# A new hand-written order of all operations, setup copies on either of two engines, and other operands for the fill matmuls

## The chip, the cores and the metric

The kernel runs on one core of a Trainium2 chip. The core has five engines that work through their own instruction streams and wait for one another by semaphores: TensorE (PE in the profile, its weight loads PEld), VectorE (DVE), ScalarE (ACT), GpSimd (POOL) and SyncE (SP), which here issues nearly all DMAs. The metric is the device time of one execution in microseconds (us); a median over runs is compared.

## The reference, cut to what matters

```python
def reference(A_u, A_*, B_*):
    x = A_u                                             # (1, 2048, 512), bf16
    h = x + S4(layernorm(x))                            # state-space convolution
    return h + mlp(layernorm(layernorm(h)))             # 512 -> 1376 -> 512

def S4(u, A, B, C, log_dt, Dskip):                      # A, B, C: complex (512, 128)
    dt = exp(log_dt)
    P = exp(dt * A[:, :, None] * arange(2048))          # arange is rounded to bf16
    K = einsum("dn,dnl,dn->dl", C, P, dt * B).real      # one kernel of 2048 taps per channel
    y = irfft(rfft(pad(u)) * rfft(pad(K)))[:2048]       # long convolution over time
    return y + u * Dskip

def mlp(y, w1, b1, w2, b2):
    return gelu(y @ w1 + b1) @ w2 + b2
```

So: 512 kernels of 2048 taps are generated from 128 complex modes each, 2048 rows are convolved with them, and an MLP of 2 x 2048 x 512 x 1376 multiply-adds follows.

## The kernel before, in words

**Setup (0 to about 45 us).** The six parameter arrays are loaded and transposed by TensorE. VectorE computes phases and logarithms of 512 channels x 128 modes in small operations; ScalarE takes exponentials of them (L724, `bexps`; L941 and L944, `aexps`, out of PSUM). GpSimd builds constants: the scaled identities `WA` (one 128x128 tensor_scalar each, 20 of them), index tables by iota and memset, and `W2`. SyncE copies the split phases into the stacked array `S2` (`restack`, 16 DMAs of 32 KB). VectorE also takes the layer norm statistics of the 16 row tiles (`BN_STATS`, L863). When ScalarE has done its last exponential it loads another function table (L501) and turns to sines.

**Kernel generation (about 45 to 97 us).** `chain` adds up phases in PSUM (L978), ScalarE takes sines of them (L980), and VectorE multiplies the exponentials by them (L999, L1000, and L985, L986 for the second half of the channels). GpSimd meanwhile masks the tables `W` (28 tensor_scalars of 128x4x32), `DD` (128x32) and others, all through the helper `PTS` (L558, recorded at L555). `kgen` (L1022, L1023) contracts over the modes for the first half of the channels; its result gets the skip weight added by VectorE (L1036), which reads `Dz`. `Dz` is loaded by four tiny DMAs on SyncE (`in_A_Dskip`, L1180). One more DMA on SyncE, of 768 KB (`ar<-ar 128x8x384`), copies padding from `EA2` to `IA2`; it may start when GpSimd has done its masks, since temporaries lie where it writes.

**Spectra (about 97 to 160 us).** `kspec` (L1087), `kgen4` (L1053, L1054), `xspec` (L885) and `fstage` (L904) are matmuls whose results ScalarE (L507) or VectorE (L509) copy out of PSUM. `kstage` sends a transposed copy through DRAM (`AK_d`). `inverse` multiplies the spectra on VectorE (L1127), transforms back on TensorE (L1137) and turns the result by a DMA transpose (L1143).

**Tail and MLP (about 160 us to the end).** `tail` (L1201, L1206) adds the residual, takes the second layer norm's statistics on VectorE (L1214, then a chain of 128x4 operations at L553 to L569), scales, and transposes (L1239); `mlp` does L1260 with a GELU on ScalarE (L1262), and L1282 with an addition on VectorE (L1284) and the output DMAs.

**What sets the order.** Every operation is recorded as an `Op` with its engines, a modelled cost and its operands. `Sched.run` walks through the list `ORDER`, a table of numbers that says in which order the 1045 operations are issued and, by a sign, on which of two engines one runs. Engines execute their own instructions in that order. `run` keeps modelled times, and where it models TensorE idle it inserts fill matmuls (`fill`, L1370 to L1372), which write a free PSUM slot. `LAG`, `OWN` and the costs at the `add` calls are the model's numbers. The key `hv` marks an operation that takes part in a mutual stop of GpSimd and VectorE. Before, a VectorE operation so marked is lengthened by a marked GpSimd operation; GpSimd is never lengthened.

Of the kernel before, what the change touches and what calls it, by code (L numbers as in the profile page):

```python
# [9 lines left out]
ACT = mybir.ActivationFunctionType  # L10
# [140 lines left out]
class VS(V):  # L151
# [12 lines left out]
LAG = {"PE": 0.12, "ACT": 0.20, "DVE": 0.14, "POOL": 0.15, "SP": 0.15}  # L164
OWN = {"PE": 0.0, "ACT": 0.17, "DVE": 0.11, "POOL": 0.1, "SP": 0.0}
ORDER = [
# [78 lines left out]
class Sched:  # L245
# [42 lines left out]
    def run(self, nslots):  # L288
        ops = self.ops
        left = {}  # L290
        for o in ops:
            for p in set(o.ps):
                left[p] = left.get(p, 0) + 1
        free = dict(FREE)
        clk, pf, lands = Clock(), 0.0, []
        slots = [0.0] * nslots
        taken = [None] * nslots
        dma_busy, bulk = 4.0, 4.0
        ipe, blk = 16, 0.0
        order, seen = [], set()  # L300
        assert sorted(i if i >= 0 else ~i for i in ORDER) == list(range(len(ops)))
# [77 lines left out]
def kernel(ctx, tc, A_u, A_A_re, A_A_im, A_B_re, A_B_im, A_C_re, A_C_im, A_log_dt, A_Dskip,  # L379
# [18 lines left out]
    pe = Pe()  # L398
# [1014 lines left out]
```

## Time and profile before

| | |
|---|---|
| median of 3 runs | 273.55 us (273.02 to 274.47) |
| the profiled execution's own time | 274.52 us |
| its span, first to last instruction | 272.7 us |
| PE busy | 234.8 us (86%), 3237 matmuls |
| DVE busy | 181.4 us (67%) |
| ACT busy | 176.8 us (65%) |
| POOL busy | 70.2 us (26%), all but one instruction in the first 86 us |
| chain that ended last | PE 57%, POOL 15%, DVE 12%, ACT 8%, DMA 4% |
| mean granted TensorE clock | 0.969 of full speed |

The chain that ended last is followed back from the last instruction, at each step to what released it. Shares of busy time are averages over stages with different limits; which engine a stage waits for is read stage by stage.

### The profile page before, as it was taken

Reading aid. Unit: us, or ns where it says so; the run is one execution under the profiler, and the core shown is the slowest. Engines: PE = TensorE matmul, PEld = TensorE weight load, DVE = VectorE, ACT = ScalarE, POOL = GpSimd, SP = SyncE. Lnnn points to the kernel's source line nnn. Section 1 sums busy time; section 2 is a strip of 40 time slices with the busy share of each in tenths; the row PEclk is TensorE's granted clock in tenths of the full one; section 3 lists DMA queues with packets and bytes.
Section 4 is the critical chain, followed back from the end, with each engine's and each line's share of the span. In section 5 each row is a group of like instructions: output and inputs, shape, how many; then the busy total and the mean of one; then the engine's idle time right before and its main releaser. Section 6 shows DMA issues by size and latency. Waiting matters only on the chain.

```text
span 272.7 us, 7643 instructions
## 1 busy us (share of the span) xinstructions
PE 234.8 (86%) x3237; PEld 134.3 (49%) x3237; DVE 181.4 (67%) x351; ACT 176.8 (65%) x214; POOL 70.2 (26%) x251
## 2 busy tenths in 40 slices
PE   6319948977885499999999988899999999999994
PEld 2206723444764358643447753655654444444452
DVE  3889996999992584278699883799538662412021
ACT  3899929999792587789899861885531561451810
POOL 8968613999996000000000000000000000000000
PEclk9999997999999599999999995999999999999999
DMA  5660010100002108696476999041254004106302
GB/s 158 158 129 11 17 48 5 3 4 2 5 2 69 54 0 266 186 306 184 144 242 183 173 155 215 2 81 25 55 102 83 19 9 80 38 0 136 78 5 72
DMA packets 40371, 23.88 MB, mean 88 GB/s; under 512 B 25649, under 2 KB 37778, under 8 KB 40338
## 3 DMA queue, kind: packets, MB, share of 16 engines
q1 hardware_dynamic: 39746, 22.95, 34.9%
q8 instruction: 25, 0.41, 0.6%
q10 hardware_dynamic: 592, 0.46, 0.6%
q14 instruction: 8, 0.07, 0.1%
HBM read 10.03 MB, written 6.29 MB: 60 GB/s over the span
## 4 chain that ended last, share of the span: by engine, by line
PE 57%; POOL 15%; DVE 12%; ACT 8%; DMA 4%; issue 2%; SPq 1%; ACTq 0%; DVEq 0%; POOLq 0%
PE ps L1260 14%; PE ps L1282 14%; POOL ar L555 13%; PE ps L1137 7%; PE ps L885 5%; PE ps L904 5%; ACT ar L507 4%; PE ps L1087 3%; DVE ar L863 3%; DVE ar L564 3%; DVE ar L569 2%; PE ps L1206 2%; DMA ar<-ar 2%; PE ps L1053 2%; DVE ar L555 2%
## 5 line engine op out<-in xcount | busy, mean ns | idle before, releaser
L507 ACT CAST ar<-ps 128x1024 bf16<-128x1024 f32 (+3 forms) x75 | 66.6, 961 | 18.9 <-DVE ar L1214 6.8
L1262 ACT ACTIVATE ar<-ps,ar 128x512 bf16<-128x512 f32 (+1 forms) x44 | 28.3, 684 | 42.3 <-PE ps L1260 41.1
L555 POOL TENSOR_SCALAR ar<-ar 128x128 bf16<-128x128 bf16 (+6 forms) x60 | 46.7, 799 | 0.4
L980 ACT ACTIVATE ar<-ps 128x1024 bf16<-128x1024 int16 x36 | 34.7, 1029 | 12.0 <-DVE ar L1000 7.2
L1260 PE MATMUL ps<-ar 128*128 128x512 bf16 (+1 forms) x176 | 40.1, 380 | 0.0
L1282 PE MATMUL ps<-ar 128*128 128x512 bf16 (+3 forms) x187 | 39.8, 367 | 0.0
L509 DVE CAST ar<-ps 128x1024 bf16<-128x1024 f32 (+3 forms) x25 | 28.7, 1162 | 15.0 <-PE ps L885 5.1
L978 PE MATMUL ps<-ar 128*32 128x256 f16 x560 | 23.2, 293 | 16.4 <-ACT ar L980 12.2
L1284 DVE TENSOR_TENSOR ar<-ps,ar 128x512 bf16<-128x512 f32 (+1 forms) x17 | 11.1, 658 | 37.1 <-PE ps L1282 19.7
L1127 DVE TENSOR_TENSOR ar<-ar 128x1024 bf16<-128x1024 bf16 x48 | 30.6, 686 | 6.3 <-PE ps L1137 6.2
L1282 PEld LDWEIGHTS <-ar 128*128 128x128 bf16 (+1 forms) x187 | 18.0, 97 | 20.3 <-issue 1.0
L978 PEld LDWEIGHTS <-ar 128*32 128x32 f16 x560 | 15.0, 101 | 25.1 <-issue 19.6
L1260 PEld LDWEIGHTS <-ar 128*128 128x128 bf16 (+1 forms) x176 | 17.3, 100 | 20.3 <-issue 0.6
L1137 PE MATMUL ps<-ar 64*128 64x128 bf16 x768 | 25.4, 223 | 1.3 <-ACT ar L507 1.1
L1137 PEld LDWEIGHTS <-ar 64*128 64x128 bf16 x768 | 22.9, 98 | 6.7 <-issue 4.0
L904 PE MATMUL ps<-ar 128*64 128x512 bf16 (+1 forms) x160 | 17.8, 342 | 0.9 <-ACT ar L507 0.8
L576 ACT ACTIVATE ar<-ar 128x512 f32<-128x512 f32 (+8 forms) x18 | 11.9, 687 | 8.6 <-DVE ar L569 5.4
L724 ACT ACTIVATE ar<-ar 128x1024 bf16<-128x1024 f32 x16 | 15.8, 1044 | 1.0 <-DVE ar L553 1.0
L885 PE MATMUL ps<-ar 128*32 128x512 bf16 x256 | 16.0, 381 | 0.0
L933 PE MATMUL ps<-ar 128*128 128x512 f16 x24 | 8.0, 460 | 8.4 <-DVE ar L553 7.4
L999 DVE TENSOR_TENSOR ar<-ar 128x1024 bf16<-128x1024 bf16 x21 | 15.0, 737 | 0.2
L569 DVE SCALAR_TENSOR_TENSOR ar<-ar 128x4 f32<-128x4 f32 (+5 forms) x44 | 12.6, 288 | 3.7 <-ACT ar L576 2.9
(100 smaller groups left out, 320.6 us busy)
## 6 DMA issues: line engine op xcount, KB each, us to landing
ar<-AK_d SPq DMA_DIRECT2D x8, 512.0 KB, 6.5
ar<-in_A_u_dram SPq DMA_DIRECT2D x4, 512.0 KB, 7.7
AK_d<-ar SPq DMA_DIRECT2D x2, 1024.0 KB, 5.5
AK_d<-ar SPq DMA_DIRECT2D x4, 512.0 KB, 3.7
out_dram<-ar SPq DMA_DIRECT2D x30, 64.0 KB, 2.1
ar<-in_B_w_dram SPq DMA_DIRECT2D x4, 344.0 KB, 5.3
ar<-in_B_w_dram SPq DMA_DIRECT2D x2, 640.0 KB, 4.9
ar<-ar SPq DMA_DIRECT2D x1, 768.0 KB
```

Source lines behind the costliest of these rows:

```text
L507: act.copy(out_fn(), in_fn())
L509: dve.tensor_copy(out_fn(), in_fn())
L555: en.tensor_scalar(a, b, f(s1), f(s2), op0, op1)
L885: pe.matmul(pst(p)[32 * cg:32 * cg + 32, 512 * z:512 * z + 512], lhsT=BD.ap()[:, 32 * f + 2 - 2 * jl:32 * f + 34 - 2 * jl], rhs=un[2 * (2 ...
L904: pe.matmul(pst(p)[64 * h:64 * h + 64, w * (k + r):w * (k + r) + w], lhsT=T.ap()[:, f, r, :], rhs=v[f:f + 1].ap()[:, 0, :], start=True, st ...
L978: pe.matmul(pst(p)[32 * g:32 * g + 32, 256 * j:256 * j + 256], lhsT=W2[DELTAS.index(d)].ap(), rhs=S2[g].ap()[:, ch0:ch0 + 256], start=Fals ...
L980: add("ACT", c_act(1024), lambda e, p=p, sc=sc, cs=cs: act.activation(swo(sc[cs]) if hf and kind == "B" else sc[cs].ap().rearrange("p a b ...
L1127: dve.tensor_tensor(o, a, b_[:, :, ::-1, :] if sw else b_, ALU.mult)
L1137: pe.matmul(pst(p)[:, 512 * h + 128 * k:512 * h + 128 * k + 128], lhsT=q.ap()[rows, 2 * k + r, :], rhs=TP[w].ap()[rows, f0 // 2 + k, :], s ...
L1260: pe.matmul(pst(p)[:fs, 512 * z:512 * z + 512], lhsT=w1s[dc].ap()[:, fc * P:fc * P + fs], rhs=ybuf.ap().rearrange("p (t c) k -> p c t k", ...
L1262: add("ACT", c_act(512, 1), lambda e, p=p, z=z, fc=fc, fs=fs: act.activation(hT.ap()[:fs, fc, :], pst(p)[:fs, 512 * z:512 * z + 512], ACT. ...
L1282: pe.matmul(pst(p)[:, 512 * z + c0:512 * z + c1], lhsT=hT.ap()[:fs, fc, 128 * t:128 * t + 128], rhs=w2s[fc].ap()[:fs, c0:c1], start=(fc == ...
```

## The change

- `ORDER` is replaced as a whole. Many setup operations that stood on GpSimd alone may now stand on VectorE, and the new table puts 17 of them there: 11 of the 20 scaled identities `WA`, one index table of 128x512, four of the 28 masks `W`, and one 128x512 subtraction (`HLg[1]`). Two copies out of PSUM of `kgen` and one of 128x512 in the setup go from VectorE to ScalarE.
- The model in `run` changes: a marked GpSimd operation now also waits for a VectorE operation under way, and pushes VectorE's next; PE's lag is 0.19 for 0.12, a DMA transpose costs 2.5 for 2.2. This acts on the instructions only through where fills are inserted: 42 instead of 30.
- Fills multiply `identb` by the raw input rows `hs[15]` throughout, as soon as both are there; before, they multiplied `I16` by a constant, and later `identb` by `TP[0]`.

```diff
-LAG = {"PE": 0.12, "ACT": 0.20, "DVE": 0.14, "POOL": 0.15, "SP": 0.15}
+LAG = {"PE": 0.19, "ACT": 0.20, "DVE": 0.14, "POOL": 0.15, "SP": 0.15}
 ORDER = [
-    15, 0, 146, 1, 11, 12, 2, 16, 28, 4, 60, 183, 155, 3, 17, 61, 18, 83, 19, 82, 63, 62, 65, 98, 64, 147, 84, 76, 5, 72, 20, 99, 8, 85, 42, 39, 104,
...
+    15, 12, 0, 1, 6, 2, 11, 60, 145, 3, 61, 183, 63, 62, 16, 65, -57, 113, 5, -44, 83, -38, 13, 185, 84, 4, 114, -48, 85, 49, 115, -52, 116, -51, 64,
...
-            if e == "DVE" and o.hv and pf > s:
-                end += min(2.6, pf - s)
+            if e == "DVE" and o.hv:
+                end += min(2.6, max(0.0, pf - s))
+                hold = hold[-15:] + [(s, end)]
             if e == "POOL" and o.hv:
-                pf = end
-            if e == "PE" and s > FILL0 and s - free[e] > 0.6 and fs:
-                t, z = max(fs[0][0], free[e], FILL0), fs[0][1]
+                for a, b in hold:
+                    if a <= s < b:
+                        s, end = b, b + c
+                late = [a for a, _ in hold if s < a < end]
+                free["DVE"] += min(2.6, end - late[0]) if late else 0.0
+                o.start, pf = s, end
+            if e == "PE" and self.src <= seen and s - free[e] > 0.6 and fs:
+                t, z = max([fs[0][0], free[e], FILL0] + [ops[d].end + 0.2 for d in self.src]), fs[0][1]
...
-                    dma_busy = max(share(end, 2.2, bulk), dma_busy)
+                    dma_busy = max(share(end, 2.5, bulk), dma_busy)
...
-        add(eng, c_dve(n, mode, psum) if eng == "DVE" else 0.25 + n / 1540.0, fn, r=r, w=[o], pr=pr, hv=1)
+        c = c_dve(n, mode, psum) + (0.08 if isinstance(s1, V) else 0.02)
+        add("DVE" if eng == "DVE" else ("POOL", "DVE"), c if eng == "DVE" else (0.25 + n / 1540.0, c), fn, r=r, w=[o], pr=pr, hv=int(not psum))
...
-    def fill(z, t):
-        w, x = (I16.ap(), cst.ap()) if t < 60 else (identb.ap(), TP[0][0:4].ap().rearrange("p a b -> p (a b)"))
-        pe.matmul(slots[z][:, 0:512], lhsT=w, rhs=x, start=True, stop=True)
+    def fill(z):
+        pe.matmul(slots[z][:, 0:512], lhsT=identb.ap(), rhs=hs[15].ap(), start=True, stop=True)
```

Lines of the changed file are 6 to 8 higher than those of before (L519 becomes L525, L1180 becomes L1188, L1127 becomes L1135).

**SyncE's queue from the restacks to the first copy to DRAM.** `ar<-ar 32x512` is a restack, `in_A_Dskip` a quarter of `Dz`, `in_B_b` the bias, `ar<-ar 128x8x384` the padding, `AK_d` the spectrum. Before:

```order
L519 DMA ar<-ar 32x512 x15
L1180 DMA ar<-in_A_Dskip_dram 1x4x32
L1180 DMA ar<-in_B_b_dram 128x10x1
L1180 DMA ar<-in_B_b_dram 96x1
L519 DMA ar<-ar 128x8x384
L1180 DMA ar<-in_A_Dskip_dram 1x4x32
L519 DMA AK_d_68<-ar 128x8x512 x2
```

After:

```order
L525 DMA ar<-ar 32x512 x6
L1188 DMA ar<-in_A_Dskip_dram 1x4x32
L1188 DMA ar<-in_B_b_dram 128x10x1
L1188 DMA ar<-in_A_Dskip_dram 1x4x32
L1188 DMA ar<-in_B_b_dram 96x1
L1188 DMA ar<-in_A_Dskip_dram 1x4x32
L525 DMA ar<-ar 128x8x384
L525 DMA AK_d_68<-ar 128x8x512 x2
```

The last quarter of `Dz`, which stood behind the padding copy, now stands ahead of it.

**VectorE at the start of the setup.** `TENSOR_SCALAR ar<-ar 128x128` at L561 is a scaled identity `WA`; rows of 128x17 and 128x1 are the field constants, those of 128x512 are on channels. Before:

```order
L564 TENSOR_TENSOR ar<-ar 128x17
L1293 MEMSET ar 128x8x192
L564 TENSOR_TENSOR ar<-ar 128x17 x3
L718 TENSOR_TENSOR ar<-ps_64,ar 128x128 x2
L564 TENSOR_TENSOR ar<-ps_64,ar 128x256
L553 TENSOR_SCALAR ar<-ar 128x512
L754 MEMSET ar 128x1
L564 TENSOR_TENSOR ar<-ps_64,ar 128x256
```

After:

```order
L1301 MEMSET ar 128x8x192
L726 TENSOR_TENSOR ar<-ps_64,ar 128x128 x2
L571 TENSOR_TENSOR ar<-ps_64,ar 128x256
L571 TENSOR_TENSOR ar<-ar 128x17
L559 TENSOR_SCALAR ar<-ar 128x512
L561 TENSOR_SCALAR ar<-ar 128x128 x3
L1184 MEMSET ar 128x64
L576 SCALAR_TENSOR_TENSOR ar<-ps_65,ar 128x512
L561 TENSOR_SCALAR ar<-ar 128x128
```

The memset no longer stands behind an operation that waits for GpSimd, and scaled identities stand between the operations on channels.

**VectorE at the second layer norm's statistics.** `BN_STATS` reads the residual sum in PSUM, the rows of 128x4 are the statistics' chain, `128x1024` is a product of spectra for `inverse`. Before:

```order
L1214 BN_STATS ar<-ps_66 128x6 x2
L1127 TENSOR_TENSOR ar<-ar 128x1024
L564 TENSOR_TENSOR ar<-ar 128x4
L1127 TENSOR_TENSOR ar<-ar 128x1024
L569 SCALAR_TENSOR_TENSOR ar<-ar 128x4
L1127 TENSOR_TENSOR ar<-ar 128x1024
L564 TENSOR_TENSOR ar<-ar 128x4
L1127 TENSOR_TENSOR ar<-ar 128x1024
L569 SCALAR_TENSOR_TENSOR ar<-ar 128x4
```

After:

```order
L1222 BN_STATS ar<-ps_67 128x6 x2
L571 TENSOR_TENSOR ar<-ar 128x4
L576 SCALAR_TENSOR_TENSOR ar<-ar 128x4
L571 TENSOR_TENSOR ar<-ar 128x4
L576 SCALAR_TENSOR_TENSOR ar<-ar 128x4
L561 TENSOR_SCALAR ar<-ar 128x4
```

The four products of 128x1024 that stood between the chain's operations stand ahead of it and behind it.

## Rows read from the trace of the kernel before

**Rows 1.** Busy time by stage (A:B, length, engines, PEclk, DMA share, GB/s)

```profile
20.00:41.00 21.00, 17.28 (x109) 11.26 (x107) 20.90 (x39) 15.51 (x19) 11.67 (x19) 1.00 0.10 25
41.00:83.60 42.60, 35.84 (x949) 23.07 (x953) 39.88 (x69) 37.94 (x45) 38.26 (x38) 0.96 0.03 4
83.60:97.00 13.40, 6.99 (x195) 4.91 (x191) 5.57 (x12) 5.70 (x6) 2.40 (x8) 0.75 0.20 61
97.00:157.00 60.00, 59.20 (x1048) 35.77 (x1038) 43.46 (x60) 52.41 (x59) 0.52 (x1) 1.00 0.70 192
157.00:182.40 25.40, 21.31 (x341) 13.60 (x338) 18.31 (x43) 14.43 (x17) 0.00 (x0) 0.87 0.57 120
182.40:269.00 86.60, 86.46 (x587) 42.15 (x587) 38.92 (x100) 36.16 (x54) 0.00 (x0) 1.00 0.26 53
```

**Rows 2.** Chain of work that ended last (start us, us, what)

```profile
77.25 8.60 POOL ar L555 x12
...
86.64 3.57 DMA ar<-in_A_Dskip_dram
...
158.91 6.02 DMA ar<-ar
```

**Rows 3.** Timeline of VectorE around the wait (start, us, instruction, idle before)

```profile
83.20 0.41 DVE L873 TENSOR_SCALAR ar<-ar 128x512 bf16<-128x512 bf16 x1
90.23 0.18 DVE L1036 TENSOR_TENSOR ar<-ar 128x32 bf16<-128x32 bf16 x1 [6.62 <-DMA ar<-in_A_Dskip_dram]
```

**Rows 4.** Timeline of SyncE's queue, same place

```profile
85.88 0.71 SPq L519 DMA_DIRECT2D ar<-ar  x1
86.64 0.65 SPq L1180 DMA_DIRECT2D ar<-in_A_Dskip_dram  x1
```

**Rows 5.** Timeline of PE: matmuls before and behind the wait

```profile
70.21 1.08 PE L978 MATMUL ps<-ar 128*32 128x256 f16 x32
...
92.20 1.96 PE L978 MATMUL ps<-ar 128*32 128x256 f16 x32 [6.01 <-ACT ar L980]
...
95.67 4.45 PE L1087 MATMUL ps<-ar 20*128 20x512 bf16 x64
```

**Rows 6.** Timeline of VectorE in the setup

```profile
7.04 0.46 DVE L553 TENSOR_SCALAR ar<-ar 128x512 f32<-128x512 f32 x1
...
20.52 1.63 DVE L564 TENSOR_TENSOR ar<-ar 128x512 f32<-128x512 f32 x1
...
24.48 2.06 DVE L555 TENSOR_SCALAR ar<-ar 128x512 f32<-128x512 f32 x1
...
29.96 1.69 DVE L555 TENSOR_SCALAR ar<-ar 128x16 int32<-128x16 int32 x1
...
34.63 0.23 DVE L569 SCALAR_TENSOR_TENSOR ar<-ar 128x16 int32<-128x16 int32 x1
...
39.68 1.25 DVE L569 SCALAR_TENSOR_TENSOR ar<-ar 128x16 f32<-128x16 f32 x1
```

**Rows 7.** Timeline of ScalarE at the end of the setup

```profile
40.96 0.55 ACT L576 ACTIVATE ar<-ar 128x16 f32<-128x16 f32 x2 [5.36 <-DVE ar L569]
```

**Rows 8.** GpSimd's groups by shape (count, busy us, mean ns, idle before)

```profile
L555 POOL TENSOR_SCALAR ar<-ar 128x128 bf16<-128x128 bf16 x28 | 27.5, 997 | 0.0
L555 POOL TENSOR_SCALAR ar<-ar 128x128 f16<-128x128 bf16 x20 | 7.0, 364 | 0.4
```

**Rows 9.** VectorE's groups by shape

```profile
L569 DVE SCALAR_TENSOR_TENSOR ar<-ar 128x512 f32<-128x512 f32 x4 | 2.8, 691 | 2.9 <-ACT ar L576 2.9
...
L1183 DVE CAST ar<-ar 128x11 f32<-128x11 bf16 x1 | 1.0, 1012 | 0.0
...
L553 DVE TENSOR_SCALAR ar<-ar 128x32 f32<-128x32 int32 x1 | 0.2, 228 | 0.0
```

**Rows 10.** Timeline of PE: fills before the tail

```profile
157.37 1.68 PE L1372 MATMUL ps<-ar 128*128 128x512 bf16 x7
```

**Rows 11.** Timeline of VectorE: a product between the statistics' operations

```profile
172.80 0.68 DVE L1127 TENSOR_TENSOR ar<-ar 128x1024 bf16<-128x1024 bf16 x1
```

More of the change, by code (lines that the diff above doesn't have):

```diff
@@ L294, in run @@
         free = dict(FREE)
-        clk, pf, lands = Clock(), 0.0, []
+        clk, pf, lands, hold = Clock(), 0.0, [], []
         slots = [0.0] * nslots
@@ L325, in run @@
                     d.i, d.e, d.start, d.deps, d.cost = -1, "PE", t, [], (0.215,)
-                    d.fn = lambda e, z=z, t=t: self.fill(z, t)
+                    d.fn = lambda e, z=z: self.fill(z)
                     t = clk.work(t, 0.215, 0.215)
@@ L538, with POOL @@
     ct = tL
-    def POOL(cost, f, r=(), w=(), pr=None, hv=0):
+    def POOL(cost, f, r=(), w=(), pr=None, hv=1):
         add("POOL", cost, lambda e: f(), r=r, w=w, pr=pr, hv=hv)
@@ L546, in TS @@
         n = n if n is not None else (o.hi - o.lo) // SZ[o.dt]
-        en = dve if eng == "DVE" else gp
         def fn(e):
+            en = dve if e == "DVE" else gp
             a = oap() if oap else o.ap()
@@ L562, in TT @@
         n = n if n is not None else (o.hi - o.lo) // SZ[o.dt]
-        en = dve if eng == "DVE" else gp
-        add(eng, c_dve(n, mode, psum) if eng == "DVE" else 0.12 + n / 480.0, lambda e: en.tensor_tensor(oap() if oap else o.ap(), aap() if aap else a.ap(), bap() if bap else b.ap(), op), r=[a, b], w=[o], pr=pr, hv=int(mode > 1))
+        c = c_dve(n, mode, psum)
+        add("DVE" if eng == "DVE" else ("POOL", "DVE"), c if eng == "DVE" else (0.2 + n / 440.0, c), lambda e: (dve if e == "DVE" else gp).tensor_tensor(oap() if oap else o.ap(), aap() if aap else a.ap(), bap() if bap else b.ap(), op), r=[a, b], w=[o], pr=pr, hv=int(not psum))
     def STT(o, a, s, b, op0, op1, n=None, psum=False, oap=None, aap=None, bap=None, pr=None):
@@ L605 @@
     POOL(0.5, ident_fn, w=[identb], pr=0)
+    S.src = {S.wr[k] for v in (identb, hs[15]) for k in S.keys(v)}
     i1 = ct(i32, 32)
@@ L1304 @@
     for c in range(2):
-        add("POOL", 0.2, lambda e, c=c: gp.memset(EB[c][16].ap(), 1.0), w=[EB[c][16]], pr=1.7)
+        add("POOL", 0.2, lambda e, c=c: gp.memset(EB[c][16].ap(), 1.0), w=[EB[c][16]], pr=1.7, hv=1)
         add("POOL", 0.2, lambda e, c=c: gp.memset(IB[c][16].ap(), 0.0), w=[IB[c][16]], pr=1.71 + 0.01 * (c // 2))
@@ L1328 @@
     for c in range(2, 4):
-        add("POOL", 0.2, lambda e, c=c: gp.memset(EB[c][16].ap(), 1.0), w=[EB[c][16]], pr=1.7)
+        add("POOL", 0.2, lambda e, c=c: gp.memset(EB[c][16].ap(), 1.0), w=[EB[c][16]], pr=1.7, hv=1)
         add("POOL", 0.2, lambda e, c=c: gp.memset(IB[c][16].ap(), 0.0), w=[IB[c][16]], pr=1.71 + 0.01 * (c // 2))
```

70 rows, old and new, of the table ORDER are left out of this document.

## The prediction

> **What bounds the kernel now.** I read the busy times by stage first, then the chain that ended last, then timelines where the chain leaves TensorE. By stage the program has two halves. From 97 us on TensorE is the bound: busy 59.20 of 60 us up to 157, and 86.46 of 86.60 us from 182.4 to the last matmul at 269 [rows 1]. Between these lies a passage of 25.4 us with TensorE busy 21.31 at 0.87 of the clock [rows 1], in which the chain goes through a DMA transpose of 6.02 us [rows 2]. Before 97 us TensorE waits for others: VectorE is busy 20.90 of the 21 us from 20 to 41, and 39.88 of the 42.6 us from 41 to 83.6, and GpSimd 38.26 in the latter [rows 1]. From 83.6 to 97 nothing is full: TensorE 6.99, VectorE 5.57, ScalarE 5.70 of 13.4 us, at a mean clock of 0.75 [rows 1].
>
> That hole is the place to read. VectorE ends an operation at 83.6 and starts the next, the addition of the skip weight, at 90.23, having waited 6.62 us for a DMA of `Dskip` [rows 3]. This tiny DMA was issued at 86.64, right behind the padding copy, issued at 85.88 [rows 4]; and this one had to wait for GpSimd, whose last run of masks ends at 77.25 + 8.60 = 85.85 [rows 2]. So a DMA that needs nothing stands in SyncE's queue behind one that needs GpSimd, and VectorE's queue, ScalarE's sines behind it and TensorE behind those (idle 6.01 us until 92.20) stand still.
>
> **The change part by part.**
>
> *Term A, SyncE's queue.* All four quarters of `Dskip` now stand ahead of the padding copy. The 6.62 us wait of VectorE goes. What is late next: the products queued behind the addition, whose sines are from ScalarE, idle in the hole too; and GpSimd's end at 85.85, since `kspec` reads all masks, but that began at 95.67 [rows 5]; 6.6 less is 89, still 3 us behind GpSimd. Value -6.6. Bounds: -6.6, and -3.3 if half is taken up by the next wait.
>
> *Term B, the clock behind the hole.* TensorE had done nothing for 6.01 us, and 32 matmuls took 1.96 us where the same 32 took 1.08 in the running chain [rows 5]: 0.88 lost. More is lost in `kspec`, which starts in the same stretch of mean clock 0.75 [rows 1]; I take 0.6 for it. If the hole is gone the matmuls run on at the full clock. Value -1.5, bounds 0 and -3.4 (a quarter of 13.4 us).
>
> *Term C, work between 45 and 97 us.* GpSimd has 24 masks and one index table of 128x512 fewer to do than its 28 and four, about 4 x 1.0 us and 1 us off its 38 [rows 1, 8]; it stays off the path by this, with a cover of some 8 us (3 us above, 5 more). VectorE gets four masks, 4 x 0.23 = 0.9 us by the nearest small tensor_scalar [rows 9], and loses two copies out of PSUM of about 0.7 each to ScalarE, which is busy 37.94 of 42.6 us and so nearly as full [rows 1]. Value -0.5, bounds -1.4 and +1.5.
>
> *Term D, the setup.* What ends it is VectorE: ScalarE idles 5.36 us, until 40.96, for the layer norm's statistics [rows 7], and only then can load its table for sines. VectorE is lengthened there by GpSimd: a tensor_scalar of 128x512 takes 2.06 us at 24.48 and 0.46 at 7.04; two operations of 128x16 take 1.69 and 1.25 where another takes 0.23 [rows 6]; a two-input operation of 128x512 takes 1.63 [rows 6] where the like takes 0.69 [rows 9]. Excess: 1.60 + 1.46 + 1.02 + 0.94 = 5.0 us. The new order puts other things beside each other there: GpSimd's reading operations stand beside statistics more often. Against this VectorE gets 11 scaled identities, 11 x 0.23 = 2.5 us [rows 9], and an index table, 0.46 us [rows 6]; the subtraction it gets and the copy it loses are of one size. Net -5.0 + 3.0 = -2.0. Bounds: -5.4, where ScalarE has no idle time left to give, and +3.0, when all the excess stays.
>
> In rows 8, the masks take GpSimd 997 ns each while VectorE is full; the scaled identities, of the same 128x128 elements, 364 ns, mostly beside other work. The Trainium skill (SBUF — State Buffer, section Who interferes with whom) says that the two engines share one pair of ports, that whichever instruction starts first holds it to its end, and that the other is blocked entirely meanwhile. By it a mask waits for one product of about 0.68 us and then takes its 0.3 to 0.4, which is what the row shows; it would also have each tensor_scalar moved to VectorE blocked for a whole GpSimd instruction whenever that started first, and the term above would be worse by as much. That is the slower rival below.
>
> *Term E, the passage from 157 to 182.4 us.* It holds idle time, 25.4 - 21.31 = 4.1 us, and fills, seven of which take 1.68 us [rows 10]. The transposes of the first half now stand together without copies between them, and four products of 0.68 us each [rows 11] leave the chain of small statistics, 2.7 us off a chain that TensorE waits for. Against that there are 12 more fills, 12 x 0.24 = 2.9 us, if the engine is not idle where they stand; and one load of the spectrum comes later than the transposes, so that the second half's `inverse` may wait for it. Value 0, bounds -4.1 and +4.1.
>
> The raw input as the fills' operand costs nothing new: the shape is the same, and the statistics of the setup read those rows too. If the first fills had to wait for them, the setup's matmuls queued behind would wait as well; that lies within the upper bound of D.
>
> Behind 182.4 the same matmuls remain on a full engine: 0.
>
> *Sum.* -6.6 - 1.5 - 0.5 - 2.0 + 0 = -10.6 on the profiled execution's 274.52 us gives 263.9. That execution lies 0.97 above the median of the runs, 273.55, so 263.0 as a median.
>
> **The rivals.**
>
> *Given back in the passage.* Everything arrives 10 us earlier, but the transposes and the copies through DRAM (DMA share 0.70 from 97 to 157, [rows 1]) don't, or the later load of the spectrum holds `inverse`. For: the passage is bound by latency, not by an engine. Against: these DMAs are issued by results that also come earlier. Price +4.1 to +5: 263.0 + 5 = 268.
>
> *GpSimd's masks become the bound.* If each of the 24 takes 1.3 us rather than 1.0, since VectorE no longer pauses, they end 24 x 0.3 = 7 us later than planned, about where they ended before, and `kspec` starts behind them at 87 to 90 instead of 85. Price +4: 267.
>
> *The setup copies clog VectorE (slower).* Seventeen operations come to VectorE, which is full until 83.6. If each meets a GpSimd instruction and takes what the cast of 11 elements took, 1.01 us [rows 9], they cost 17 us rather than 4, and if the 5.0 us of excess stay too, the sum is -6.6 - 1.5 + 17 + 1 = +10: 283. It decides from a mean of about 0.5 us for each, where with the excess kept the gains of A and B are used up. Against it: the ones placed late stand between products, which GpSimd waits for rather than the reverse.
>
> *The change doesn't do what it says.* The hole closes at `Dskip` and opens at the next wait, and the setup is as long as before: then only B or nothing is left, 272 to 274.
>
> **How the numbers follow.** Forecast 263.0, own range 258 to 267.5, chance 0.62. Given back in the passage: 0.15. GpSimd's masks: 0.08. No change: 0.07. Slower: 0.08. What a measurement of this kernel can tell from no change is about 0.5%, 1.4 us. Faster: 0.62 + 0.15 + 0.08 = 0.85; same 0.07; slower 0.08. The range goes down to A, B and D at their far ends and up past the first two rivals: 256.5 to 270.
>
> **What would show it right or wrong.** A is right if VectorE's addition of the skip weight has no wait for a `Dskip` DMA, and `kspec` starts before 89 us; wrong if another wait of over 3 us stands in VectorE's row between 75 and 90. B: no stretch with a clock of 0.75 ahead of `kspec`. C: GpSimd ends at 78 to 82 us. D: ScalarE's wait for the statistics ends at about 39 instead of 40.96 us, and the scaled identities on VectorE average under 0.3 us. E: the stretch from the last product ahead of the first tail to the MLP's first matmul is about as long as before, and from there to the end it is 86 to 91 us. The prediction fails if the first MLP matmul starts later than 175 us.

## The result, and the profile after

The changed kernel takes 262.50 us (median of 4 runs, 262.43 to 263.84) against 273.37 us of the kernel before (4 runs). The ratio is 0.9607, 95% interval 0.9566 to 0.9649; every ratio here is to the kernel before, run beside it. Run again later it took 263.68 us (6 runs), ratio 0.9642 (0.9597 to 0.9688). 263.0 was predicted. In some executions TensorE's granted clock falls for some us behind `kspec` (to 0.66 from 84 to 97 us in the profile of experiment 9), and the slowest of those runs are left out of the ratios (not of the medians). In the changed kernel's program L1036 of before is L1044, L1087 is L1095, L1260 is L1268, L1127 is L1135; in some experiments lines stand one further down.

The stages of the changed kernel first, as in [rows 1] (stretch, its length, busy time of PE, PEld, DVE, ACT, POOL, then PEclk, DMA share, GB/s):

```profile
84.00:97.00 13.00, 12.12 (x232) 9.54 (x231) 10.71 (x18) 11.42 (x14) 0.00 (x0) 1.00 0.41 131
...
150.00:172.00 22.00, 20.22 (x306) 12.50 (x303) 19.80 (x47) 14.08 (x19) 0.00 (x0) 1.00 0.66 145
```

The stretch ahead of 97 us, where TensorE was busy 6.99 of 13.40 us at 0.75 of the clock, now has 12.12 of 13.00 at full clock, and the passage ahead of the MLP idles 1.8 of 22.0 us instead of 4.1 of 25.4 [rows 1], though with 23 fills in it where there were 16, so that its idle time alone says little. The whole profiled execution has a span of 260.1 us (272.7 before) and a mean clock of 0.999.

VectorE's timeline (start, us, instruction; a bracket would name an idle time before it) has no wait at the first addition of the skip weight, which came at 90.23 behind 6.62 us of waiting [rows 3]:

```profile
79.20 0.26 DVE L1044 TENSOR_TENSOR ar<-ar 128x32 bf16<-128x32 bf16 x1
...
84.66 0.18 DVE L1044 TENSOR_TENSOR ar<-ar 128x32 bf16<-128x32 bf16 x1
```

SyncE's queue: the last quarter of `Dskip` is issued at 43.79, the padding copy, which still waits for GpSimd, at 82.04; before, they went at 86.64 and 85.88 [rows 4]:

```profile
43.79 0.57 SPq L1188 DMA_DIRECT2D ar<-in_A_Dskip_dram  x1
...
82.04 0.73 SPq L525 DMA_DIRECT2D ar<-ar  x1
```

On TensorE `kspec` starts at 84.90 instead of 95.67 [rows 5], the first tail no longer waits 2.20 us for a DMA transpose, and the MLP's first matmul comes at 169.85 instead of 182.32. Its timeline before, at the first tail and the MLP:

```profile
164.98 0.64 PE L1206 MATMUL ps<-ar 128*64 128x512 bf16 x2 [2.20 <-DMA ar<-ar]
...
182.32 3.63 PE L1260 MATMUL ps<-ar 128*128 128x512 bf16 x16
```

And after (L1379 are fills):

```profile
84.90 1.04 PE L1095 MATMUL ps<-ar 20*128 20x512 bf16 x16
...
155.22 0.39 PE L1209 MATMUL ps<-ar 128*128 128x512 bf16 x1
...
160.28 0.61 PE L1379 MATMUL ps<-ar 128*128 128x512 bf16 x2
160.82 1.96 PE L1145 MATMUL ps<-ar 64*128 64x128 bf16 x64
...
169.85 2.33 PE L1268 MATMUL ps<-ar 128*128 128x512 bf16 x10
```

So 10.8 us are gained by `kspec` and 1.7 between it and the MLP in these two executions (that of before lay 0.97 us above its median); from the MLP to the end it is 90.3 us, before 90.4.

The setup: ScalarE's wait for the statistics ends at 39.35 instead of 40.96 [rows 7]:

```profile
39.35 0.31 ACT L583 ACTIVATE ar<-ar 128x16 f32<-128x16 f32 x1 [1.50 <-DVE ar L576]
```

VectorE's first product of the kernel generation comes 1.72 us earlier. Before and after:

```profile
49.17 1.29 DVE L999 TENSOR_TENSOR ar<-ar 128x1024 bf16<-128x1024 bf16 x2
```

```profile
47.45 1.30 DVE L1007 TENSOR_TENSOR ar<-ar 128x1024 bf16<-128x1024 bf16 x2
```

But VectorE's lengthened operations [rows 6] did not go; they are others now:

```profile
6.67 1.87 DVE L559 TENSOR_SCALAR ar<-ar 128x512 f32<-128x512 f32 x1
...
11.88 1.33 DVE L559 TENSOR_SCALAR ar<-ar 128x512 f16<-128x512 f32 x1
...
26.16 2.27 DVE L576 SCALAR_TENSOR_TENSOR ar<-ar 128x512 f32<-128x512 f32 x1
...
31.33 1.26 DVE L576 SCALAR_TENSOR_TENSOR ar<-ar 128x512 f16<-128x512 f32 x1
```

The groups by shape (count, busy us, mean ns, idle before) of GpSimd's masks and of the identities that VectorE took over, which answer to [rows 8]:

```profile
L561 POOL TENSOR_SCALAR ar<-ar 128x128 bf16<-128x128 bf16 x24 | 26.4, 1113 | 7.3 <-ACT ar L583 7.3
```

```profile
L561 DVE TENSOR_SCALAR ar<-ar 128x128 f16<-128x128 bf16 x11 | 3.0, 368 | 0.0
```

A mask takes 1113 ns where it took 997, and an identity 368 ns on VectorE.

### The profile page after: what moved, and what is told of

Read it like the earlier page. It is cut to its first block, busy times and chain, and to the rows that moved or that the text cites. A ratio compares the mean times of both kernels' runs of the same rounds, so it can differ in the third digit from the quotient of the medians.

```text
span 260.1 us, 7656 instructions
## 1 busy us (share of the span) xinstructions
PE 230.3 (89%) x3236; PEld 133.7 (51%) x3249; DVE 183.3 (70%) x368; ACT 176.8 (68%) x214; POOL 61.8 (24%) x234
## 4 chain that ended last, share of the span: by engine, by line
PE 57%; DVE 25%; ACT 11%; issue 5%; POOL 0%; DVEq 0%; ACTq 0%; POOLq 0%
PE ps L1268 15%; PE ps L1290 15%; PE ps L1145 8%; PE ps L893 5%; ACT ar L988 4%; ACT ar L513 4%; DVE ar L871 4%; PE ps L912 4%; DVE ar L1007 3%; DVE ar L576 3%; DVE ar L571 2%; PE ps L1095 2%; PE ps L1061 2%; DVE ar L1008 2%; DVE ar L559 2%
## 5 line engine op out<-in xcount | busy, mean ns | idle before, releaser
L513 ACT CAST ar<-ps 128x1024 bf16<-128x1024 f32 (+3 forms) x72 | 65.2, 970 | 19.3 <-PE ps L1145 6.9
L561 POOL TENSOR_SCALAR ar<-ar 128x128 bf16<-128x128 bf16 (+6 forms) x44 | 39.6, 921 | 7.6 <-ACT ar L583 7.3
L1268 PE MATMUL ps<-ar 128*128 128x512 bf16 (+1 forms) x176 | 39.3, 379 | 0.0
L515 DVE CAST ar<-ps 128x1024 bf16<-128x1024 f32 (+2 forms) x28 | 30.6, 1113 | 11.9 <-ACT ar L513 4.0
L1135 DVE TENSOR_TENSOR ar<-ar 128x1024 bf16<-128x1024 bf16 x48 | 30.7, 687 | 10.3 <-PE ps L1145 9.9
L1268 PEld LDWEIGHTS <-ar 128*128 128x128 bf16 (+1 forms) x176 | 17.3, 100 | 20.5 <-issue 0.8
L986 PE MATMUL ps<-ar 128*32 128x256 f16 x560 | 21.4, 275 | 5.0 <-ACT ar L988 3.1
L1145 PEld LDWEIGHTS <-ar 64*128 64x128 bf16 x768 | 21.6, 94 | 5.4 <-issue 3.0
L1145 PE MATMUL ps<-ar 64*128 64x128 bf16 x768 | 23.9, 217 | 0.3 <-ACT ar L513 0.3
L986 PEld LDWEIGHTS <-ar 128*32 128x32 f16 x560 | 14.3, 97 | 12.5 <-issue 12.2
L576 DVE SCALAR_TENSOR_TENSOR ar<-ar 128x4 f32<-128x4 f32 (+5 forms) x44 | 14.2, 327 | 2.5 <-ACT ar L583 1.4
L1008 DVE TENSOR_TENSOR ar<-ar 128x1024 bf16<-128x1024 bf16 x21 | 14.6, 719 | 0.0
L1007 DVE TENSOR_TENSOR ar<-ar 128x1024 bf16<-128x1024 bf16 x21 | 14.5, 716 | 0.1
```

The source lines that it names most:

```text
L513: act.copy(out_fn(), in_fn())
L515: dve.tensor_copy(out_fn(), in_fn())
L561: en.tensor_scalar(a, b, f(s1), f(s2), op0, op1)
L986: pe.matmul(pst(p)[32 * g:32 * g + 32, 256 * j:256 * j + 256], lhsT=W2[DELTAS.index(d)].ap(), rhs=S2[g].ap()[:, ch0:ch0 + 256], start=Fals ...
L1135: dve.tensor_tensor(o, a, b_[:, :, ::-1, :] if sw else b_, ALU.mult)
L1145: pe.matmul(pst(p)[:, 512 * h + 128 * k:512 * h + 128 * k + 128], lhsT=q.ap()[rows, 2 * k + r, :], rhs=TP[w].ap()[rows, f0 // 2 + k, :], s ...
```

## The experiments

Numbers in `ORDER` are operations: 192 is the DMA of the last quarter of `Dskip`, 341 the padding copy. A negative entry is an operation on the second of its two engines: -57 is operation 56, and so on.

**1. The kernel before, Dskip first.**

```diff
 ORDER of before
-  ..., 375, 253, 341, 373, ..., 395, 192, 424, ...
+  ..., 375, 253, 192, 341, 373, ..., 395, 424, ...
```

> The kernel before, with one change: the last quarter of Dskip is issued on SyncE right ahead of the padding copy instead of behind it. Theory (terms A and B): the addition of the skip weight loses its 6.62 us wait and runs at about 83.6 us, kspec starts at 88 to 89 instead of 95.67, no stretch with a clock of 0.75 is left ahead of it; 273.4 - 6.6 - 1.5 = 265.3 us, ratio 0.970. Rival 1 (the next wait takes half of it: GpSimd's masks still end at 85.85 here): kspec at 92, 270 us, ratio 0.988. Rival 2 (the gain of the changed kernel came from the moved setup and mask work, not from the queue): another wait of over 5 us before 90 us, 272 to 274 us.

Measured: 266.96 us (6 runs) against 273.46, ratio 0.9764 (0.9726 to 0.9802), so 6.5 us (5.4 to 7.5). VectorE's, GpSimd's and TensorE's timelines:

```profile
83.72 0.17 DVE L1037 TENSOR_TENSOR ar<-ar 128x32 bf16<-128x32 bf16 x1
```

```profile
77.42 10.47 POOL L556 TENSOR_SCALAR ar<-ar 128x32 bf16<-128x32 f32 x12
```

```profile
88.87 4.09 PE L1088 MATMUL ps<-ar 20*128 20x512 bf16 x64
...
93.83 0.29 PE L1055 MATMUL ps<-ar 128*128 128x132 bf16 x1 [0.66 <-DMA ar<-ar]
...
158.54 0.44 PE L1207 MATMUL ps<-ar 128*64 128x512 bf16 x2 [2.06 <-DMA ar<-ar]
```

The addition moves by 6.51 us, `kspec` by 6.80: on VectorE no other wait takes the place of the first. Term A is right to 0.1 us. GpSimd's last masks take 10.47 us where they took 8.60 [rows 2], now beside a VectorE that does not pause, and end 1 us ahead of `kspec`. Through the padding copy they are the next bound all the same: it is issued when they have ended, at 87.92, and `kgen4`'s second matmul (L1055) waits 0.66 us for it, until 93.83. Before, `kgen4` began at 100.05 and had no such wait. What the queue does not give is the other 3.3 to 4.3 us of the change (0.9764 less 0.9642 or 0.9607, of 273.4 us). This wait is a small part of it: in the changed kernel the copy goes at 82.04, and `kgen4`, from 90.68 on, waits for nothing.

**2. The changed kernel, Dskip last.**

```diff
 ORDER of after
-  364, 425, 248, 192, 367, ..., 237, 249, 424, 383, 394, 341, 395
+  364, 425, 248, 367, ..., 237, 249, 341, 192, 424, 383, 394, 395
```

> The changed kernel, with the last quarter of Dskip put back behind the padding copy on SyncE. The padding copy can go at 82.0 us, when GpSimd's last mask ends, and Dskip lands some 4.4 us behind it, at 86.4. Theory (A and B): the first addition of the skip weight, now at 79.20 without a wait, waits until 86.4, so 7.2 us, and TensorE's clock falls behind the hole; 262.5 + 7.2 + 1.0 = 270.7 us, ratio to the kernel before 0.990. Rival 1 (the queue was not the cause; work order elsewhere was): under 264.5 us, ratio under 0.968. Rival 2 (half is taken up, since kspec waits for other things until 84.90 anyway): 266, ratio 0.973.

Measured: 269.7 us, ratio 0.9866 (0.9829 to 0.9903); 6.1 to 7.1 us slower than the changed kernel by the ratios. VectorE's timeline and the stage:

```profile
83.41 0.17 DVE L1045 TENSOR_TENSOR ar<-ar 128x32 bf16<-128x32 bf16 x1 [4.96 <-issue]
```

```profile
85.00:95.00 10.00, 7.72 (x112) 3.61 (x115) 9.01 (x16) 6.99 (x8) 0.00 (x0) 0.66 0.01 2
```

The hole is back and the clock falls to 0.66 of full speed behind it. The row names no releaser ("issue"), but the addition starts 3.64 us behind the issue of `Dskip` at 79.77, as it did before (90.23 less 86.64, 3.59 us). In this execution GpSimd ended 3 us earlier than expected (padding copy at 78.99), 2.1 us of them by a setup that came out shorter (last section), and so the wait is 4.96 and not 7.2; it is the fastest of the six. From `kspec` to the first matmul of `kgen4` it is 6.8 us against 5.8 in the changed kernel: 1.0 us for the clock. Undoing and doing the one move agree: it carries 60 to 66% of the gain (6.5 of 10.9 or 9.8 us).

**3. The setup's moves undone.** 13 operations back on GpSimd, at their places.

```diff
 ORDER of after
-  -57 -44 -38 -48 -52 -51 -46 -49 -43 -53 -47   -104   -257
+   56  43  37  47  51  50  45  48  42  52  46    103    256
```

> The changed kernel, with 13 setup operations put back from VectorE to GpSimd at the same places of the order: 11 scaled identities, one 128x512 index subtraction, one index table. Theory (term D as predicted: the moves cost VectorE some 3.0 to 4.5 us, the gain came from placing): VectorE is relieved, GpSimd has 10 us of idle time from 15.5 to 25.7 us, and ScalarE's wait for statistics ends at 36.5 to 37.5 us instead of 39.35; 260.5 us, ratio 0.953. Rival 1 (the moves are what kept GpSimd from stopping VectorE): the lengthened operations of VectorE grow by more than the 4.5 us taken off; the wait ends at 41 or later, 264 to 265 us, ratio 0.967 to 0.970. Rival 2 (a setup of another length is taken up before the first product): within 0.7 us of 262.5.

Measured: 265.05 us, ratio 0.9708 (0.968 to 0.9736), 1.8 to 2.8 us slower. GpSimd's, VectorE's and ScalarE's timelines:

```profile
20.19 1.16 POOL L571 TENSOR_TENSOR ar<-ar 128x512 f16<-128x512 f32 x1 [7.63 <-DVE ar L559]
...
29.18 3.38 POOL L571 TENSOR_TENSOR ar<-ar 128x928 f32<-128x928 f32 x2
```

```profile
33.34 0.18 DVE L571 TENSOR_TENSOR ar<-ar 128x16 f32<-128x16 f32 x1
...
40.90 1.47 DVE L561 TENSOR_SCALAR ar<-ar 128x16 int32<-128x16 int32 x4
```

```profile
32.60 0.72 ACT L583 ACTIVATE ar<-ar 128x512 f32<-128x512 f32 x1 [2.02 <-POOL ar L571]
```

The time is close to rival 1's, and what sets it is neither's mechanism. VectorE is relieved at first, as the theory says: its chain behind the statistics starts at 33.34 instead of 36.80 (up to 2.1 of these 3.5 us may be another thing, told in the last section). But it ends at 42.37, in the changed kernel at 42.18: beside GpSimd's later work these small operations take 9.0 us instead of 5.4, which is the lengthening of rival 1. Nor is VectorE what ScalarE waits for here. GpSimd's queue stops for 7.63 us at the subtraction that it got back, which needs VectorE; memsets and index tables stand behind it, the product of 128x928 begins at 29.18 instead of 25.73, and ScalarE waits 2.02 us for it. The move of that one subtraction is thus again a matter of what stands behind a waiting instruction. (That it alone does it was not tried.)

**4. The four masks back on GpSimd** (-233, -234, -253, -254 become 232, 233, 252, 253).

> The changed kernel, with the four masks that it puts on VectorE back on GpSimd (28 there, as before). Theory (VectorE sets the start of kspec, since kspec stands 0.23 us behind the second addition of the skip weight in before, after and the run with Dskip first, whether GpSimd ends 3 us ahead or 1): VectorE loses 4 x 0.30 = 1.2 us, the second addition comes at 83.5 instead of 84.66, GpSimd's masks end at 82.0 + 4 x 1.1 = 86.4, the total is 261.3 to 262.5 us, ratio 0.956 to 0.960. Rival (GpSimd's masks are the bound, as in the second rival of the prediction): kspec starts at 87 to 87.5 behind the masks, 264.5 to 265 us, ratio 0.968. Rival 2 (four more reading operations on GpSimd stop VectorE by what they no longer take from it): same as the changed kernel within 0.7 us.

Measured: 262.77 us, ratio 0.9632 (0.9593 to 0.9671): no difference. GpSimd's and TensorE's timelines:

```profile
84.03 1.59 POOL L562 TENSOR_SCALAR ar<-ar 128x128 bf16<-128x128 bf16 x2
```

```profile
85.50 1.04 PE L1096 MATMUL ps<-ar 20*128 20x512 bf16 x16
```

GpSimd's last two masks end at 85.62, and `kspec` has started by then, at 85.50, just 0.6 us later than in the changed kernel: GpSimd does not set `kspec`'s start, and the masks' move was worth nothing by itself. VectorE did not come earlier either, so the theory's gain of 1.2 us fails as well.

**5. No fills** (`FILLN = 0` instead of 24).

> The changed kernel without any fill matmul. Theory (the fills keep the granted clock up in the setup and in the passage of 150 to 165 us, where TensorE otherwise waits): a stretch at the lower level of 1.2 GHz appears at 15 to 45 us or behind 165 us; 264 to 268 us, ratio 0.966 to 0.98. Rival (the fills end behind the results that TensorE waits for and delay it): 261 to 262 us, ratio under 0.958. Rival 2 (neither): within 0.7 us of 262.5.

Measured: 262.88 us, ratio 0.9643 (0.9595 to 0.9691): rival 2, no difference. The passage's stage without them:

```profile
150.00:172.00 22.00, 16.52 (x297) 11.65 (x292) 19.23 (x44) 14.36 (x18) 0.00 (x0) 0.92 0.72 161
```

TensorE is busy 16.52 instead of 20.22 us and its clock is 0.92: 64 matmuls of `inverse` take 3.35 us at 160.90 where they took 1.96. Yet the MLP's first matmul comes at 170.25, only 0.4 us later. So the fills that were added, and their new operand, have no part in the gain, and the passage's higher clock (1.00 after, 0.87 before) has at most a small one.

**6. The four products back in the chain of statistics** (808 to 811; of `ORDER` only VectorE's operations are shown here and in 7, and in 7 TensorE's 812).

```diff
 ORDER of after
-  808 809 679 810 681 811 684 686     688     689     690     691 ...
+          679     681     684 686 811 688 808 689 809 690 810 691 ...
```

> The changed kernel, with four products of the second half's inverse (0.68 us each) put back between the first operations of the chain of small statistics of the first tail, as they stood before. Theory (term E: the chain ends late and TensorE waits for it): the chain from the last BN statistics to the scaling takes 2.7 us more, 5.3 instead of 2.6; the MLP's first matmul comes 2.4 to 2.7 us later at about 172.4, 264.9 to 265.2 us, ratio 0.970. Rival 1 (the inverse's matmuls, which wait for the same products, gain what the chain loses, or other work covers it): within 0.7 us of 262.5. Rival 2 (half): 263.7.

Measured: 265.5 us, ratio 0.9735 (0.9689 to 0.9782), 2.5 to 3.5 us slower. VectorE's and TensorE's timelines:

```profile
159.85 0.69 DVE L1136 TENSOR_TENSOR ar<-ar 128x1024 bf16<-128x1024 bf16 x1
...
161.20 0.69 DVE L1136 TENSOR_TENSOR ar<-ar 128x1024 bf16<-128x1024 bf16 x1
...
163.39 0.56 DVE L577 SCALAR_TENSOR_TENSOR ar<-ar 128x4 f32<-128x4 f32 x3
165.37 0.69 DVE L1136 TENSOR_TENSOR ar<-ar 128x1024 bf16<-128x1024 bf16 x1 [1.43 <-PE ps L1146]
```

```profile
160.36 3.41 PE L1380 MATMUL ps<-ar 128*128 128x512 bf16 x15
163.71 1.96 PE L1146 MATMUL ps<-ar 64*128 64x128 bf16 x64
...
171.68 3.63 PE L1269 MATMUL ps<-ar 128*128 128x512 bf16 x16
```

The time is the theory's, the way is only in part. The chain of statistics itself ends at 163.95 instead of 163.07. The scaling behind it (L1238) starts 2.4 us later, at 165.98 instead of 163.59, because one more product stands ahead of it that waits 1.43 us for the inverse's matmuls, which start at 163.71 instead of 160.82. They need the four products, the last of which ends at 161.89; from then to 163.7 TensorE is still in fills, 15 where there were two. So up to 1.8 us of the delay are fills, and what the products' place costs without them was not tried. The MLP starts 1.8 us later in this execution.

**7. The same in the kernel before**, on top of experiment 1: products and the matmuls that use them put behind the chain.

```diff
 ORDER of before
-  811 688 808 689 809 690 810 691 ... 699 812 700 ... 701 702
+      688     689     690     691 ... 699     700 ... 701 702 811 808 809 810 812
```

> The kernel before with Dskip first (264.4 to 267.9 us, median 266.96), and with the same four products and the inverse's matmuls that use them put behind the chain of small statistics of the first tail, where they stood between its operations. Theory (term E): from the last BN statistics to the scaling it was 7.2 us (163.6 to 170.8 us in the run with Dskip first), now 3 to 4; the MLP's first matmul comes 1.7 to 3 us earlier, at 172.7 to 174; 264 to 265.3 us, ratio 0.966 to 0.970. Rival 1 (the gain of the passage lies elsewhere: in the transposes that stand together, or in the DMA that the first tail waits 2.06 us for): the chain is shorter, but the first MLP matmul stays at 175 to 176, 266.5 to 267.5 us. Rival 2 (the products, now later, hold up the second half): 268 or more.

Measured: 269.07 us, ratio 0.9878 (0.9825 to 0.9931), about 3 us slower than experiment 1: rival 2. VectorE's and TensorE's timelines:

```profile
166.39 2.49 DVE L1128 TENSOR_TENSOR ar<-ar 128x1024 bf16<-128x1024 bf16 x4
172.62 0.69 DVE L1128 TENSOR_TENSOR ar<-ar 128x1024 bf16<-128x1024 bf16 x1 [3.74 <-PE ps L1138]
173.23 0.73 DVE L1230 TENSOR_SCALAR ar<-ar 128x512 bf16<-128x512 bf16 x2
```

```profile
168.59 2.32 PE L1373 MATMUL ps<-ar 128*128 128x512 bf16 x10 [1.10 <-ACT ar L508]
170.84 1.96 PE L1138 MATMUL ps<-ar 64*128 64x128 bf16 x64
```

The small chain ends at 166.47 instead of 169.02, but ahead of the scaling (L1230) stands one more product in VectorE's queue, which waits 3.74 us for TensorE's inverse, now at 170.84 instead of 168.42. So products merely taken out of the chain gain nothing: what stands ahead of the scaling still waits for the inverse, and that for them. Here too the four products end (168.88) while TensorE is in fills, ten of them, so up to 2.0 us of the loss may be theirs. That the products have to be ahead of the chain, as in the changed kernel, is likely but not shown by itself.

**8. New setup, old rest; and 9. new up to `kspec`, old rest.** The code after, with the first 233 or 435 entries of its `ORDER`, and all others in the order of experiment 1.

```diff
 ORDER of after
+  first 233 (435) entries as they are,
+  then what is left, in the order of before with 192 ahead of 341
```

> The changed kernel's code and its order up to the first product of the chain (47.45 us), and from there on the order of the kernel before with Dskip first. Theory (D is worth 1.7 to 1.9 us by itself): the first product at 47.4 to 47.8 us and everything behind as in the run with Dskip first (median 266.96): 265.1 to 265.3 us, ratio 0.970. Rival 1 (what the setup gains is taken up behind it, GpSimd's masks being no earlier): 266.5 to 267, ratio 0.976. Rival 2 (the setup is worth more, since GpSimd starts its masks earlier too): under 264.3, ratio under 0.967.

> The changed kernel's code and its order up to kspec (84.90 us), and from there on the order of the kernel before. Theory (C is small at 0.3 to 0.5 us, E is the rest): kspec starts at 84.9 to 85.2, the first tail waits about 2 us for its transpose again, the chain of small statistics has the four products in it, the MLP's first matmul comes 2 to 3 us later than 169.85; 264.5 to 265.5 us, ratio 0.968 to 0.971. Rival 1 (the gain of the passage came from the earlier arrival, not from its order): 262.5 to 263.2 us, ratio 0.960 to 0.963. Rival 2 (the old order fits the new arrivals badly): 266.5 or more.

Measured: the first 268.49 us, ratio 0.9815 (0.9763 to 0.9867); by the ratios 1.4 us slower than experiment 1, which the two intervals do not tell apart, and not faster as the theory has it. VectorE's timeline in its fastest run:

```profile
62.05 1.29 DVE L1009 TENSOR_TENSOR ar<-ar 128x1024 bf16<-128x1024 bf16 x2 [1.27 <-ACT ar L989]
...
78.77 0.79 DVE L995 TENSOR_TENSOR ar<-ar 128x1024 bf16<-128x1024 bf16 x1 [0.97 <-ACT ar L989]
```

Here the first product comes at 45.40, but between it and the addition VectorE waits for ScalarE's sines again and again, 2.9 us in all. In the changed kernel there is no such wait, and in experiment 2, whose first product came as early (45.33), 0.9 us. What the setup gains is taken up behind it unless the generation is ordered anew too (rival 1). The seam is a cost of this experiment as well, so it gives no price for D alone.

The second: 267.8 us, ratio 0.9686 (0.9617 to 0.9755). Its two best runs are 263.43 and 263.92 us, the changed kernel's two best in the same series 262.33 both; its third at a clock of over 0.99 took 266.25. TensorE's timeline has the old wait of the first tail again:

```profile
161.89 0.41 PE L1215 MATMUL ps<-ar 128*64 128x512 bf16 x2 [2.01 <-DMA ar<-ar]
```

So the new order behind `kspec` is worth about 1.1 to 1.6 us by the best runs (1.2 by the ratios). That lies between the theory and rival 1 (nothing), which the interval does not exclude.

**10. GpSimd's memsets later**, in the changed kernel (26: 128x514, 32: 128x512, 142: the other 51).

```diff
 ORDER of after
-  81 44 26 -43 ... 38 128 32 73 ... 167 142 76 ... 106 146 107
+  81 44    -43 ... 38 128    73 ... 167     76 ... 106 146 26 32 142 107
```

> The changed kernel, with a block of GpSimd memsets (128x512, 128x928, 44 of one column, 6 of four) moved from 6.9 to 10 us to behind the last index memset, into GpSimd's idle time from 15.5 us on. In the changed kernel a tensor_scalar of VectorE of 128x512 takes 1.87 us at 6.67 beside two tensor_scalars and then these memsets, where one alone takes 0.46. Theory (the memsets hold VectorE, though they read nothing): it takes under 0.9 us, the ScalarE exponential behind it starts at 7.3 instead of 8.57, and the total is 0.5 to 1.4 us less: 261.1 to 262, ratio 0.955 to 0.958. Rival 1 (the two reading GpSimd operations at 6.43 hold it, or any that follow): it still takes over 1.4 us, the total within 0.5 us of 262.5. Rival 2 (it is shorter, but the setup's end is set by VectorE's work later on): shorter operation, ScalarE's wait for statistics still ends at 39.3, same total.

Measured: 261.74 us, ratio 0.9574 (0.9542 to 0.9605). Run once more, beside the changed kernel itself:

> The changed kernel once more, on the chip and beside the runs of before that the next kernel shares: 262.4 to 263.8 us, ratio 0.960. The tensor_scalar of 128x512 at 6.67 takes 1.87 us and ScalarE's exponentials start at 8.57 as in four profiles so far, if the hold is no accident of one execution.

> The changed kernel with the block of GpSimd memsets moved to 15.5 us, once more, for a direct comparison with the changed kernel in the same call. Theory (the memsets' hold of VectorE at 6.67 delays the whole setup): 0.6 to 1.4 us faster than the changed kernel, 261.1 to 261.9 us, ratio 0.955 to 0.958. Rival (the earlier difference of 0.76 us was between chips): within 0.4 us of the changed kernel.

Measured: the changed kernel 263.68 us, ratio 0.9642 (0.9597 to 0.9688); with the memsets later 262.1 us, ratio 0.9586 (0.9542 to 0.9631). The means of six runs each are 263.34 and 261.81, a difference of 1.5 us with an interval of about 1 to either side (from the runs' spread). It is the fastest version, by little. Its VectorE timeline:

```profile
6.72 0.54 DVE L560 TENSOR_SCALAR ar<-ar 128x512 f32<-128x512 f32 x1
```

The operation takes 0.54 us instead of 1.87, the first product comes at 46.00 instead of 47.45, and the span is 258.6 us instead of 260.1: the whole 1.5 us reach the end.

## Why the prediction was right, and where not

**A, SyncE's queue (-6.6): right.** Experiment 1 shows 6.5 us, by the way described, and experiment 2 the reverse. What is late next was called wrongly, at little cost. `kspec` does not wait for all masks: in experiment 4 it starts at 85.50, and the last two end at 85.62. What waits for GpSimd's end is `kgen4`, through the padding copy, 0.66 us in experiment 1.

**B, the clock (-1.5): too large.** Behind the hole `kspec` gains 0.3 us more than the addition, and the stretch from it to `kgen4` is 4.02 us instead of 4.38; with experiment 2's 1.0 us for that stretch, B is 0.65 to 1.0. The step that failed is "I take 0.6 for it" (`kspec`), which measured 0.36, and the 0.88 us of slow matmuls, of which 0.3 reached `kspec`: it stands 0.23 us behind VectorE's second addition with the hole and without. Experiment 1 gave 6.5 us in all and not the 8.1 of A and B, as 6.5 + 0.65 - 0.66 for the new wait adds up.

**C, work from 45 to 97 us (-0.5): far too small.** From VectorE's first product to `kspec` it was 46.50 us before, 39.52 with Dskip first, and is 37.45 in the changed kernel: 2.1 us less than the queue alone gives, outside the bounds of C (-1.4 to +1.5). The masks that moved are worth nothing (experiment 4); the two copies that went to ScalarE were not tried alone. So it is the order, as far as is known: experiment 8 shows that with the old order of the generation VectorE waits 2.9 us for ScalarE. The step that failed is that C counts only the work moved between engines and puts the order of what stays at nothing. GpSimd's end at 82.0 us was called rightly.

**D, the setup (-2.0): the size right (-1.7 at the first product), both parts of it wrong, so the size is luck.** That 5.0 us of excess would go was wrong: by the rows above the four operations exceed the like ones by 1.41 + 0.87 + 1.58 + 0.57 = 4.4 us (0.46 for the tensor_scalars, 0.69 for the others). The identities were put at 2.5 us and kept VectorE busy for 3.0; at 0.368 us each on average their sign (under 0.3 us) failed. In two of eight executions of this order the setup came out 2.1 us shorter still (last section). Experiment 3 shows VectorE's statistics done 1.4 to 3.5 us earlier without the 13 moves, about their price of 3.0, but also what pays for them: without them GpSimd stops in its queue, its work falls beside VectorE's small operations, and all is 2 to 3 us slower.

**E, the passage (0): too small.** From `kspec` to the MLP it gained 1.7 us in the profile, of which 0.36 are B's, and 1.1 to 1.6 us by experiment 9. The bound of -4.1 held it. The step that failed was the choice of the middle, with 2.9 us of added fills against the gain: in the changed kernel fills cost nothing (experiment 5). Which part of the order pays is open. Putting the products back costs 2.5 to 3.5 us (experiment 6), but with up to 1.8 us of fills in it; the transposes that now stand together, and with which the first tail's wait of 2.20 us went, were not tried alone. The sign, a stretch "about as long as before" at the first tail, failed: from the tail's first matmul to the MLP's it is 14.6 us instead of 19.9. Most of that is work that now stands ahead of the tail, since from `kspec` to the tail it is 70.3 us instead of 66.7.

So by the two profiles the MLP starts 12.5 us earlier: A 6.5, B 0.65, C 2.25, D 1.7 and E 1.3 (C against the kernel before itself). The sum said 10.6, and the medians gained 9.8 to 10.9, less than this pair of executions. That 263.0 lies so near the median is in part luck: B was some 0.85 us too large and D 0.3, C 1.75 too small and E 1.3. Of the rivals, GpSimd's masks did become longer (1113 ns, 1.3 us were feared), but did not become the bound of the changed kernel. "Slower" needed VectorE's moved operations at 0.5 us and more each; the identities took 0.37. "Given back in the passage" had the sign wrong: the passage gained.

## What to carry to other kernels

Look first for an instruction that needs nothing and stands in a queue behind one that waits: one DMA moved by a few places was worth some 60% of a change that reordered 1045 operations. Then look for what waits for the same thing by another way: here the copy that stood ahead of that DMA waits for GpSimd as well, and cost 0.66 us at the next stage (experiment 1). When a stage is to gain, order the next one for its new arrival, or the gain turns into waits there (experiment 8). A fill is worth nothing where TensorE waits anyway (experiment 5), and an experiment on the order moves the fills too: look whether a result is ready while they still run (experiments 6 and 7).

## What the runs showed of the hardware

GpSimd's memsets, which read nothing, held up VectorE, as far as the rows show. In the changed kernel VectorE's tensor_scalar starts at 6.67 and ends at 8.54, while GpSimd's timeline is this:

```profile
6.43 0.56 POOL L561 TENSOR_SCALAR ar<-ar 128x128 f16<-128x128 bf16 x2
6.93 0.53 POOL L657 MEMSET ar<- 128x512 f16 x1
7.39 0.87 POOL L807 MEMSET ar<- 128x928 f32 x1
8.32 1.53 POOL L811 MEMSET ar<- 128x1 f32 x44
```

GpSimd's last reading operation ends at 6.99, and until 8.54 only memsets follow. In experiment 2, with the same order here and starts within 10 ns, VectorE's operation took 0.41 us, and GpSimd's pair 0.81:

```profile
6.44 0.81 POOL L562 TENSOR_SCALAR ar<-ar 128x128 f16<-128x128 bf16 x2
```

In the changed kernel's profile, its repeat and experiments 4, 5, 6 and 9 GpSimd got ahead (ScalarE's exponentials at 8.57); in 2 and 8 VectorE did (7.13 and 7.12), with the first product at 45.33 and 45.40 instead of 47.45. Two outcomes of one order thus lie 2.1 us apart. Experiment 10 took the memsets away and VectorE's operation was short in both its profiles, but it also got ahead there, by 0.02 us, of the reading GpSimd operation that came in their place (6.72 and 6.74); so it shows what the hold is worth and not that a memset holds where another operation would not. The Trainium skill (SBUF — State Buffer, section Who interferes with whom) says that GpSimd and a VectorE instruction in one of its two-port modes contend for a shared pair of ports, and that whichever of the two issues first has it for the whole instruction. The trace agrees that it is one or the other; that VectorE waits through several GpSimd instructions in a row, 1.4 us, the rule does not say.
